# Adding the low word of a float64 weight to the bits of a float32 as an integer

## The chip, the cores and the metric

The kernel runs on one core of a Trainium2 chip. The metric is the device time of one execution in microseconds. The engines are named as in the profile: PE is TensorE, PEld its weight load, DVE is VectorE, ACT is ScalarE, POOL is GpSimd, SP is SyncE, which issues the DMAs.

## The reference

```python
X = np.fft.rfft(x, axis=1)                  # x: 2 x 3008 x 256, float32
Y = X * (filt_r + 1j * filt_i)[None]        # the filter: 1505 x 256
x = np.fft.irfft(Y, n=3008, axis=1).astype(np.float32).reshape(6016, 256)
h = x @ moe_w_in                            # 256 x 2048
x = ((np.maximum(h, 0) + alpha * np.minimum(h, 0)) @ moe_w_out).astype(np.float32)
h = np.maximum(x @ moe2_w_in, 0.0)
return (h * h @ moe2_w_out).astype(np.float32)
```

The four weight matrices (256 x 2048 and 2048 x 256) arrive as float64: a float32 array was divided by a float64 square root.

## The kernel before, in words

The convolution of each batch is an FFT of length 3008 = 64 x 47 as matmuls (units of 16 channels, lines 229 to 289, and a last stage, `stage4`, lines 297 to 314). Two networks follow, m = 0 and m = 1, on six tiles of 512 or 448 tokens per batch. The hidden dimension is cut into 16 blocks f of 128. Each operand of a network's matmul is split into a high part, rounded to the fp32r type, and a low part, the rest; a product is three matmuls (high x high, high x low, low x high).

One **step** of the main loop is one (network, batch, tile, f): six matmuls of line 423 for the hidden block (`h_mm`), the activation (`h_act`: line 436 on ACT and line 437 on DVE in the first network, lines 439 and 440 on ACT in the second), the split of the result (`g_split`: line 453 on ACT, line 454 on DVE), and two steps later six matmuls of lines 468 to 470 (`o_mm`). Tiles come in pairs: after the first few steps of the program, which take f = 0 and 1 for one tile and then for the other, each f is used for the pair's two tiles, so a new f is needed every second step. `split_x` (lines 401 and 403) makes the xs operand of a tile out of the convolution's X.

`weights(m, f)` turns 128 x 512 float64 weights into float32 and splits them. Line 320 loads a block into a staging tile stg (five of them); a view of it gives the low and the high words. Line 327 scales the low words by 2^-52 on ACT, writing floats over them. Line 329 takes the absolute value of the high words, read as floats, into c; line 331 clamps it, line 333 shifts the bits by three and masks, line 335 puts the sign and the top exponent bit of the high word back. c is then a float32 whose last three mantissa bits are zero. Line 337 masks c's exponent (and sign) into s, line 339 multiplies that by the scaled low words, line 342 adds the product to c. Line 346 rounds c to the high part (Wh for the first network) on ACT, line 348 subtracts it for the low part (Wl), and line 354 stores both to DRAM on SP's queue, from where `fetch` (line 364) loads them each time the network in the Wh and Wl tiles changes. c and s come from the nine tf tiles.

The order on every engine is written out at build time by a small planner, `Order`: each task is a generator that yields the cost of its next instruction on an engine, the events that it needs and the tiles that it takes; the planner issues, among the tasks that fit, the one that can start first. Engines run their instructions in the order so written. Before the main loop it runs until the first tile's xs and the weights f = 0 to 3 (`EARLY`) are there, and fills TensorE with `warm`, matmuls on zeros (line 505), meanwhile. In the main loop it fills each step with other tasks up to a few microseconds ahead of TensorE (lines 549 to 562): the rest of stage 4 of batch 0 at first, weights f = 4 to 15, then the second network's weights and the convolution of batch 1. Where a step needs weights that aren't planned yet, it plans their tasks first (`h_mm`).

Of the kernel before, what the change touches and what calls it, by code (L numbers as in the profile page):

```python
# [14 lines left out]
AF = mybir.ActivationFunctionType  # L15
ALU = mybir.AluOpType
# [43 lines left out]
def f32v(ap):  # L60
    return ap.bitcast(F32)
# [80 lines left out]
def conv_mlp_mlp(ctx, tc, x, fil, wts, alp, cst, out):  # L142
    nc = tc.nc
    V, A, G, T, SP = nc.vector, nc.scalar, nc.gpsimd, nc.tensor, nc.sync
# [172 lines left out]
    def weights(m, f, after=()):  # L317
        _, end = yield {"S": 0.6}, after, [(stg, 1)]
        t = stg.take()
        SP.dma_start(t.bitcast(U32), wts[m, :, f * 1024:(f + 1) * 1024])  # L320
        mark(("w", m, f), od.moved(end, 128 * 4096))
        w = t.bitcast(U32).rearrange("p (n w) -> p w n", w=2)
        low, high = w[:, 0, :], w[:, 1, :]
        yield {"A": 0.6}, [("w", m, f)], [(tf, 2)]
        c_, s_ = tf.take(), tf.take()
        c, s = c_.bitcast(U32), s_.bitcast(U32)
        A.activation(f32v(low), low, AF.Copy, scale=2.0 ** -52)
        yield {"A": 0.6}, [], []
        A.activation(c_, f32v(high), AF.Abs)
        yield {"V": 0.41}, [], []  # L330
        V.tensor_scalar(c_, c_, TINY, HUGE, op0=ALU.max, op1=ALU.min)
        yield {"V": 0.41}, [], []
        V.tensor_scalar(c, c, 3, 0x3FFFFFFF, op0=ALU.logical_shift_left, op1=ALU.bitwise_and)
        yield {"V": 0.67}, [], []
        V.scalar_tensor_tensor(c, high, 0xC0000000, c, op0=ALU.bitwise_and, op1=ALU.bitwise_or)  # L335
        yield {"V": 0.41}, [], []
        V.tensor_scalar(s, c, 0xFF800000, None, op0=ALU.bitwise_and)
        _, end = yield {"V": 0.68}, [], []
        V.tensor_mul(s_, s_, f32v(low))
        stg.give(end, t)  # L340
        _, end = yield {"V": 0.68}, [], []
        V.tensor_add(c_, c_, s_)  # L342
        tf.give(end, s_)
        _, end = yield {"A": 0.53}, [], [(tr, 2)] if m else []
        h, l = (tr.take(), tr.take()) if m else (WH[f], WL[f])
        A.copy(h, c_)  # L346
        _, end = yield {"V": 0.68}, [], []
        V.tensor_sub(l, c_, f32v(h))  # L348
        tf.give(end, c_)
        if not m:  # L350
            mark(("W", 0, 0, f), end)
        for k, p in enumerate((h, l)):
            _, end = yield {"S": 0.6}, [], []
            SP.dma_start(WD[m][f][k], f32v(p))
            end = od.moved(end, 128 * 2048)
            if m:
                tr.give(end, p)
        mark(("WD", m, f), end)
# [148 lines left out]
    with tc.manual_schedule():  # L507
# [12 lines left out]
        od.add(*(c0.stage4(h, g) for g in range(3) for h in range(2)))  # L520
        od.add(split_x(0, 0, 0), split_x(0, 0, 1))
        od.add(*(weights(0, f) for f in range(EARLY)))
        ahead, late = [], [("WD", 1, NF - 4)]
        for u in range(NU):
# [11 lines left out]
        c0.bank.give(0.0, banks[7])  # L536
        tf.keep, tr.keep = KEEP_F, KEEP_R
        od.add(*(weights(0, f) for f in range(EARLY, NF)))
        od.add(*(c0.stage4(h, g) for g in range(3, 8) for h in range(2)))
        od.add(*(split_x(*k) for k in units[2:]), lead=1.0)  # L540
        od.add(*(weights(1, f, [("W", 0, 0, NF - 1), ("xs", 0, 0, 3)]) for f in range(NF)))
        od.add(*ahead)
        t5 = len(TILES) - 1
# [99 lines left out]
```

## Time and profile before

| | |
|---|---|
| runs of the kernel | 1172.55, 1174.91, 1175.22 us (median 1174.91) |
| profiled execution | 1174.51 us, of which the span is 1172.7 us |
| mean granted TensorE clock | 0.996 |
| PE busy | 1153.8 us (98%) |
| DVE busy | 679.6 us (58%), 1067 instructions |
| ACT busy | 707.2 us (60%), 1258 instructions |
| POOL busy | 46.1 us (4%) |

The span goes from the first instruction to the last; the rest of the execution's time lies around it. Busy times count overlaps of an engine's own instructions once, so that a row's listed duration can be longer than the distance to the next instruction's start. Matmul ends are modelled. In a row of instructions the time in front is the start in microseconds from the span's start; an idle time in brackets stands with what ended it.

### The profile page before, as it was taken

The page shows a single profiled execution, that of the slowest core. Times are in us where ns is not written, and L with a number is a line of the kernel's source. Part 1 is how long each engine was busy: PE and PEld are TensorE (multiplying, and loading weights), DVE is VectorE, ACT ScalarE, POOL GpSimd, SP SyncE. Part 2 cuts the span into 40 slices and gives each one's busy share as a digit, 9 for nine tenths or more (in the row PEclk, how much of TensorE's full clock was granted, in tenths as well). Part 3 has the DMA queues.
Part 4 walks back from the last instruction along what each step waited for, and adds up shares of the span by engine and source line. Part 5 has one row for each costly group of instructions (what it writes and reads, how often), then busy time and mean ns, then how long its engine had stood idle before and what let it go on. Part 6 is the DMA issues. An engine that isn't in the chain of part 4 may idle for free.

```text
span 1172.7 us, 14233 instructions
## 1 busy us (share of the span) xinstructions
PE 1153.8 (98%) x5196; PEld 951.7 (81%) x5198; DVE 679.6 (58%) x1067; ACT 707.2 (60%) x1258; POOL 46.1 (4%) x52
## 2 busy tenths in 40 slices
PE   9999979999999999999999999999999999999998
PEld 4568658888888888888888888888888888888887
DVE  6788867888887776277622555655655322322322
ACT  1366636556667667666666644544544767767765
POOL 5400000000000110001000000000000000000000
PEclk9999989999999999999999999999999999999999
DMA  7653313323654122021223200000123100000000
GB/s 217 188 195 112 125 63 131 94 91 122 198 179 144 50 54 77 1 66 30 78 85 104 92 1 1 1 1 1 52 92 109 36 1 1 36 1 1 37 1 34
DMA packets 38007, 85.02 MB, mean 72 GB/s; under 512 B 4400, under 2 KB 5168, under 8 KB 37936
## 3 DMA queue, kind: packets, MB, share of 16 engines
q1 hardware_dynamic: 37936, 84.10, 22.3%
q8 instruction: 41, 0.67, 0.2%
q14 instruction: 30, 0.25, 0.1%
HBM read 61.15 MB, written 22.94 MB: 72 GB/s over the span
## 4 chain that ended last, share of the span: by engine, by line
PE 92%; DVE 3%; DMA 2%; ACT 1%; issue 1%; POOL 1%; POOLq 0%; ACTq 0%; SPq 0%
PE bank L423 43%; PE bank L468 14%; PE bank L470 14%; PE bank L469 14%; PE bank L308 2%; DMA stg<-in_fil 1%; PE bank L218 1%; PE bank L225 1%; PE bank L223 1%; PE bank L224 1%; DVE Wl L348 1%; DVE tf L437 1%; DVE tf L335 0%; DVE tf L342 0%; ACT tf L436 0%
## 5 line engine op out<-in xcount | busy, mean ns | idle before, releaser
L423 PE MATMUL bank<-xs,Wh 128*128 128x512 f32 (+1 forms) x1536 | 472.0, 388 | 4.1 <-ACT Wh L346 4.1
L454 DVE TENSOR_TENSOR tr<-tf,tr 128x512 fp32r<-128x512 f32 (+1 forms) x384 | 263.2, 685 | 352.9 <-ACT tr L453 348.7
L423 PEld LDWEIGHTS bank<-xs,Wh 128*128 128x128 f32 x1536 | 286.4, 188 | 58.4 <-ACT Wh L346 6.3
L453 ACT CAST tr<-tf 128x512 fp32r<-128x512 f32 (+1 forms) x384 | 234.9, 612 | 118.8 <-DVE tf L437 114.3
L423 PE MATMUL bank<-xs,Wl 128*128 128x512 f32 (+1 forms) x768 | 297.8, 388 | 5.7 <-DVE Wl L348 5.7
L468 PE MATMUL bank<-tr,Wh 128*128 128x512 f32 (+1 forms) x768 | 299.0, 389 | 0.0
L470 PE MATMUL bank<-tr,Wh 128*128 128x512 f32 (+1 forms) x768 | 297.3, 387 | 0.0
L469 PE MATMUL bank<-tr,Wl 128*128 128x512 f32 (+1 forms) x768 | 296.8, 386 | 0.0
L439 ACT ACTIVATE tf<-bank 128x512 f32<-128x512 f32 x192 | 113.2, 590 | 151.4 <-PE bank L423 151.2
L437 DVE SCALAR_TENSOR_TENSOR tf<-tf,one_minus_alpha,bank 128x512 f32<-128x512 f32 x192 | 141.3, 736 | 81.0 <-ACT tf L436 79.2
L436 ACT ACTIVATE tf<-bank 128x512 f32<-128x512 f32 x192 | 113.3, 590 | 120.3 <-PE bank L423 120.0
L423 PEld LDWEIGHTS bank<-xs,Wl 128*128 128x128 f32 x768 | 144.5, 188 | 36.1 <-DVE Wl L348 9.2
L470 PEld LDWEIGHTS bank<-tr,Wh 128*128 128x128 f32 x768 | 144.6, 188 | 27.8 <-DVE tr L454 0.3
L468 PEld LDWEIGHTS bank<-tr,Wh 128*128 128x128 f32 x768 | 144.7, 188 | 26.0
L469 PEld LDWEIGHTS bank<-tr,Wl 128*128 128x128 f32 x768 | 144.9, 189 | 25.7
L440 ACT ACTIVATE tf<-tf 128x512 f32<-128x512 f32 x192 | 119.7, 623 | 6.1
L200 POOL TENSOR_TENSOR stg<-stg,cst 128x384 f32<-128x384 f32 x32 | 30.5, 955 | 497.4 <-DMA Wl<-w 292.2
L308 PEld LDWEIGHTS bank<-cst,X 128*128 128x128 f32 x256 | 37.5, 190 | 8.3 <-ACT X L312 2.8
L287 DVE STREAM_TRANSPOSE X<-bank 128x512 f32<-128x512 f32 x32 | 34.7, 1089 | 11.1 <-PE bank L225 5.5
L403 DVE TENSOR_TENSOR xs<-X,xs 128x512 fp32r<-128x512 f32 (+1 forms) x48 | 32.5, 676 | 14.2 <-ACT xs L401 12.3
L308 PE MATMUL bank<-cst,X 128*128 128x94 f32 x256 | 36.8, 268 | 2.8 <-ACT X L312 2.2
L243 DVE STREAM_TRANSPOSE tf<-bank 128x512 f32<-128x512 f32 x32 | 22.8, 714 | 10.8 <-PE bank L218 6.9
(56 smaller groups left out, 573.6 us busy)
## 6 DMA issues: line engine op xcount, KB each, us to landing
stg<-in_wts SPq DMA_DIRECT2D x32, 512.0 KB, 4.0
stg<-in_fil SPq DMA_DIRECT2D x32, 384.0 KB, 3.5
Wh<-w SPq DMA_DIRECT2D x48, 256.0 KB, 2.6
Wl<-w SPq DMA_DIRECT2D x48, 256.0 KB, 2.9
w<-tr SPq DMA_DIRECT2D x32, 256.0 KB, 2.0
stg<-in_x SPq DMA_DIRECT2D x16, 384.0 KB, 4.2
out<-tf SPq DMA_DIRECT2D x20, 256.0 KB, 2.2
w<-Wh SPq DMA_DIRECT2D x16, 256.0 KB, 2.0
```

Source lines behind the costliest of these rows:

```text
L287: V.transpose(self.us[h].rearrange("p (i u d) -> p u d i", i=PR, u=8)[:, u % 8], pad(ps))
L308: T.matmul(ps[:, i * 94:i * 94 + 94], src[:, q], cs[:, O4:NCST], start=True, stop=True)
L423: T.matmul(ps[:, :n], w, r, start=(j == 0), stop=(j == 5))
L436: A.activation(q[:, :n], ps, AF.Relu, scale=-1.0)
L437: V.scalar_tensor_tensor(p[:, :n], q[:, :n], oma[:, f:f + 1], ps, op0=ALU.mult, op1=ALU.add)
L439: A.activation(q[:, :n], ps, AF.Relu)
L440: A.activation(p[:, :n], q[:, :n], AF.Square)
L453: A.copy(gh[:, :n], p[:, :n])
L454: V.tensor_sub(gl[:, :n], p[:, :n], f32v(gh[:, :n]))
L468: T.matmul(ps[:, :n], WH[f][:, w], gh[:, :n], start=(f == 0), stop=False)
L469: T.matmul(ps[:, :n], WL[f][:, w], gh[:, :n], start=False, stop=False)
L470: T.matmul(ps[:, :n], WH[f][:, w], gl[:, :n], start=False, stop=(f == NF - 1))
```

## The change

The low word, scaled by 2^-29, is an integer of 0 to 8 once it is rounded: what the three empty mantissa bits of c lack, with a carry. Line 327 now writes it as an integer into s, and one addition on the 32-bit patterns of c and s stands in place of mask, product and float sum. The staging tile is given back after line 335 instead of after line 339, and the planner's costs follow the new instructions.

```diff
-        A.activation(f32v(low), low, AF.Copy, scale=2.0 ** -52)
+
+        A.activation(s, low, AF.Copy, scale=2.0 ** -29)
         yield {"A": 0.6}, [], []
         A.activation(c_, f32v(high), AF.Abs)
...
-        yield {"V": 0.67}, [], []
+        _, end = yield {"V": 0.67}, [], []
         V.scalar_tensor_tensor(c, high, 0xC0000000, c, op0=ALU.bitwise_and, op1=ALU.bitwise_or)
-        yield {"V": 0.41}, [], []
-        V.tensor_scalar(s, c, 0xFF800000, None, op0=ALU.bitwise_and)
-        _, end = yield {"V": 0.68}, [], []
-        V.tensor_mul(s_, s_, f32v(low))
         stg.give(end, t)
-        _, end = yield {"V": 0.68}, [], []
-        V.tensor_add(c_, c_, s_)
+        _, end = yield {"V": 0.69}, [], []
+
+        V.tensor_add(c, c, s)
         tf.give(end, s_)
```

## Rows read from the trace of the kernel before

**Rows 1.** The page, busy us, share of the span and instructions of each engine

```profile
PE 1153.8 (98%) x5196; PEld 951.7 (81%) x5198; DVE 679.6 (58%) x1067; ACT 707.2 (60%) x1258; POOL 46.1 (4%) x52
```

**Rows 2.** Stretches of 20 us: length, busy by engine, PEclk, DMA share, GB/s

```profile
140.00:160.00 20.00, 14.56 (x53) 10.32 (x51) 15.91 (x30) 9.41 (x16) 0.00 (x0) 0.91 0.15 54
160.00:180.00 20.00, 17.32 (x66) 13.09 (x65) 12.24 (x21) 7.97 (x14) 0.00 (x0) 0.91 0.32 109
180.00:200.00 20.00, 20.00 (x90) 16.57 (x89) 16.00 (x27) 13.34 (x24) 0.00 (x0) 1.00 0.29 105
```

**Rows 3.** Waits of PE from 66 to 178 us: total us, times, longest

```profile
PE bank L423 <- DVE Wl L348: 5.7, 8, 1.5
PE bank L423 <- ACT Wh L346: 4.1, 3, 3.1
PE bank L308 <- ACT X L312: 2.2, 2, 1.5
```

**Rows 4.** PE's timeline: first matmuls of steps (start us, us)

```profile
93.29 0.71 PE L423 MATMUL bank<-xs,Wh 128*128 128x512 f32 x2
...
96.93 0.71 PE L423 MATMUL bank<-xs,Wh 128*128 128x512 f32 x2
...
110.21 0.62 PE L423 MATMUL bank<-xs,Wh 128*128 128x512 f32 x2
...
112.93 0.62 PE L423 MATMUL bank<-xs,Wh 128*128 128x512 f32 x2
...
121.09 0.61 PE L423 MATMUL bank<-xs,Wh 128*128 128x512 f32 x2
...
178.65 0.62 PE L423 MATMUL bank<-xs,Wh 128*128 128x512 f32 x2
```

**Rows 5.** Groups by line: count, busy us, mean ns, idle before

```profile
L337 DVE TENSOR_SCALAR tf<-tf 128x512 uint32<-128x512 uint32 x32 | 13.4, 421 | 0.0
L339 DVE TENSOR_TENSOR tf<-tf,stg 128x512 f32<-128x512 f32 x32 | 21.9, 685 | 0.0
L342 DVE TENSOR_TENSOR tf<-tf,tf 128x512 f32<-128x512 f32 x32 | 21.9, 685 | 0.0
L209 DVE TENSOR_TENSOR tr<-tf,tr 128x384 fp32r<-128x384 f32 x32 | 18.1, 567 | 2.1 <-ACT tr L207 1.6
L327 ACT ACTIVATE stg<-stg 128x512 f32<-128x512 uint32 x32 | 21.5, 673 | 1.5 <-DMA stg<-in_wts 1.5
```

**Rows 6.** DVE's timeline from 144.7 us (start us, us)

```profile
144.74 0.42 DVE L331 TENSOR_SCALAR tf<-tf 128x512 f32<-128x512 f32 x1
145.08 0.69 DVE L339 TENSOR_TENSOR tf<-tf,stg 128x512 f32<-128x512 f32 x1
145.68 0.69 DVE L454 TENSOR_TENSOR tr<-tf,tr 128x512 fp32r<-128x512 f32 x1
146.28 0.68 DVE L342 TENSOR_TENSOR tf<-tf,tf 128x512 f32<-128x512 f32 x1
146.89 0.74 DVE L437 SCALAR_TENSOR_TENSOR tf<-tf,one_minus_alpha,bank 128x512 f32<-128x512 f32 x1
147.54 0.42 DVE L333 TENSOR_SCALAR tf<-tf 128x512 uint32<-128x512 uint32 x1
```

**Rows 7.** DVE's and PE's timeline ahead of the main loop

```profile
56.54 0.41 DVE L337 TENSOR_SCALAR tf<-tf 128x512 uint32<-128x512 uint32 x1
...
63.33 0.70 DVE L403 TENSOR_TENSOR xs<-X,xs 128x512 fp32r<-128x512 f32 x1
...
71.84 0.69 DVE L348 TENSOR_TENSOR Wl<-tf,Wh 128x512 fp32r<-128x512 f32 x1 [0.68 <-ACT Wh L346]
...
61.44 6.85 PE L505 MATMUL bank<-zeros 128*128 128x512 bf16 x31
...
68.50 0.70 PE L423 MATMUL bank<-xs,Wh 128*128 128x512 f32 x2
```

**Rows 8.** Waits of ACT from 68 to 178 us: total us, times, longest

```profile
ACT tf L436 <- PE bank L423: 26.0, 22, 3.4
```

## The prediction

> **What bounds the kernel now.** I read the page's busy shares first: TensorE is busy 1153.8 of 1172.7 us, VectorE only 58% of it [rows 1]. So a change on VectorE and ScalarE can only be worth what TensorE loses by waiting or by filler work. The table of 20 us stretches finds the first part of that: all loss lies before 180 us, and from 140 to 180 us TensorE is busy 14.56 and 17.32 of 20 us at a granted clock of 0.91 [rows 2]; from 180 us on every stretch is full, as the third row. The waits of TensorE in 66 to 178 us then name what is late: the matmuls of line 423 wait 5.7 us in 8 waits for Wl (line 348) and 4.1 us for Wh (line 346), and the stage-4 matmuls of line 308 wait 2.2 us for a copy on ScalarE [rows 3]. Wl and Wh of the first network are what weights() delivers, so the disputed work is on the path that sets the end.
>
> What these waits cost I take from the step starts, since a wait also leaves an empty pipeline and a low clock behind. An undisturbed step is 112.93 - 110.21 = 2.72 us. From 121.09 to 178.65 us there are 15 steps (16 to 30, counted on the timeline), 57.56 us where 15 x 2.72 = 40.80 would do: **16.8 us lost** [rows 4]. One f has two steps, and eight f (8 to 15) wait, as the 8 waits say.
>
> Why is Wl late? VectorE's timeline shows when each instruction gives way to the next, which is shorter than its listed duration: a tensor_scalar 0.34 us, a two-tensor instruction 0.60, line 437 0.65 [rows 6]. One f takes two steps of lines 437 and 454 (2 x 1.25 = 2.50 us) and one block of weights: three tensor_scalar (1.02) and four two-tensor instructions (2.40), together 5.92 us. TensorE needs 2 x 2.72 = 5.44 for the same f. **In the short steps VectorE is the slower of the two by 0.48 us per f**; in the earlier long steps, with stage 4 between them (96.93 - 93.29 = 3.64 us, 7.28 per f), it gains 1.36 per f, and that lead is used up at f = 8.
>
> The second part is the start. The main loop can't be earlier than 31 warm-up matmuls allow, 6.85 us from 61.44 us (0.221 each) [rows 7]. Their number is not a wait: the planner writes as many as fit until, in its own costs, blocks 0 to 3 are done. The last xs part of the first tile starts at 63.33 us on VectorE and takes 0.70, so the data are there some 4 us before the warm-up ends [rows 7].
>
> **The change part by part.** *Removed:* line 337 (421 ns, 32 of them) and line 339 (685 ns, 32) [rows 5], in giving-way time 0.34 + 0.60 = 0.94 us per block [rows 6].
>
> *Replaced:* the float sum of line 342 becomes a sum of two uint32 tiles. No row shows that instruction. Low end: like a single-source one, 421 ns. High end within one instruction: each word taken as two 16-bit halves, 1024 elements instead of 512. From 128x384 at 567 ns and 128x512 at 685 ns an element costs 118/128 = 0.92 ns, so 685 + 512 x 0.92 = 1157 ns [rows 5]. I take 685 ns, because the instruction has the same two sources, destination and words as line 342 now. Toward the low end nothing more is won, since TensorE is the slower one by then; the high end is a rival.
>
> The Trainium skill, VectorE: DVE Perf Modes, section Specifications, says that the engine computes in float32, that integer operands are converted and that results are exact only below 2^24. By that an exact sum of 32-bit patterns can't be one plain pass; no row here shows either. One pass that rounds would give the time of the sum below; several passes give the slower rival.
>
> *Kept but redirected:* the ScalarE copy of line 327 writes s, as an integer, and no longer overwrites the low words. Nearest row: 673 ns for the same 512 columns out of uint32 [rows 5]. I cost it at nothing, and what covers it is ScalarE's idle time, 26.0 us of waiting for TensorE at line 436 alone in 68 to 178 us [rows 8]. Its ends are 0 and, at twice the duration and without that cover, 0.67 us once, in the start's last block.
>
> *Moved:* stg is given back after line 335, two or more instructions earlier, so the weight loads of line 320 on SyncE's queue can go earlier, ahead of the line 354 stores they stand between. ScalarE waits for such a load once at line 327, 1.5 us [rows 5]. I take nothing for it, with 0 and -1.5 as ends. No wait is added.
>
> *The written order:* the planner's VectorE cost of a block falls from 3.94 (0.41 + 0.41 + 0.67 + 0.41 + 3 x 0.68) to 2.86 (0.41 + 0.41 + 0.67 + 0.69 + 0.68), by 1.08. With 2 x (0.75 + 0.62) = 2.74 for two steps, a plan for one f was 6.68 against a planned 5.2 of TensorE, and is now 5.60.
>
> **Term 1, the start.** From 56.54 to 71.84 us VectorE runs practically without a gap and holds lines 337 and 339 of all four early blocks [rows 7]. Planned, that is 4 x 1.08 = 4.3 us, 19 or 20 warm-ups; really 4 x 0.94 = 3.7 us. As the first data already lie some 4 us ahead of the end of the warm-up and come earlier too, the plan's number decides. I take 4.0, with 3.5 to 4.3 as ends; what could eat into it is the tail of block 3, cast on ScalarE and then line 348, with less other work around it.
>
> **Term 2, the stalls.** VectorE's need per f falls to 5.92 - 0.94 = 4.98 us, below TensorE's 5.44. In the long steps the lead grows by 2.3 us instead of 1.4 per f, in the short ones it should no longer shrink. In the plan it still shrinks by 0.4 per f, some 3 us over eight f, which the larger lead of the long steps covers. I leave 2 us for waits at the last f's, since the instructions stand in a fixed order and a block's tail can stand behind a line 437 that waits for TensorE: 16.8 - 2 = 14.8 us back.
>
> **Term 3,** the 2.2 us at line 308 during steps 0 to 2: the copy there stands behind block 3's cast and a weight load; both come earlier by about as much as the steps do. Nothing, with 0 to -2.2 as ends.
>
> What is late next: nothing after 180 us waits now, so the time saved stays saved; work of the second convolution and the second network's weights moves with the steps.
>
> **The sum,** against the profiled execution, 1174.5 us (span 1172.7 plus 1.8 around it, 0.4 below the median of 1174.9): 1174.5 - 4.0 - 14.8 = **1155.7 us**. All ends favourable: 1174.5 - 4.3 - 16.8 - 2.2 = 1151.2.
>
> **The rivals.**
> *Half the stalls stay.* The order is written out, so an instruction free to run stands behind one that waits. For it: VectorE is busy only 12.24 of 20 us from 160 to 180 us, where Wl is latest [rows 2], so not raw capacity alone makes it late. Against it: that idleness comes after TensorE stopped, a consequence. 1174.5 - 4.0 - 8.4 = 1162.1.
> *The sum takes two half-words per word.* Giving way after about 1.07 us (1157 less the 0.085 us by which 685 exceeds 0.60), VectorE's f is 4.98 - 0.60 + 1.07 = 5.45, level with TensorE's 5.44. A third of the stalls, 5.6 us, would stay: 1174.5 - 4.0 - 11.2 = 1159.3.
> *Slower: the exact sum is several passes.* Place: between line 335 and the cast of line 346, on VectorE. What it replaces gave way after 0.34 + 0.60 + 0.60 = 1.54 us, so above that each block is slower than before. With four two-tensor passes, 2.40 us, it is 0.86 more per block, 12 x 0.86 = 10.3 us over blocks 4 to 15, while some 2 us of the start would still be won: 1183 us. The page named above speaks for it; the planner's cost of 0.69 in the diff, that of one pass, speaks against it.
> *It does nothing to the end:* Wl is late for another reason, such as its loads. The one 1.5 us wait for a load says no. 1174.5.
>
> **How the numbers follow.** Forecast 0.65, half the stalls 0.20, two half-words 0.07, nothing 0.03, several passes 0.05. A measurement can tell 0.3% here, 3.5 us; the first three cases all lie beyond it. So faster 0.92, same 0.03, slower 0.05. The range goes from 1151 (all ends favourable) to 1163 (half the stalls with the start's low end, 1162.6); the predicted time is the forecast's, rounded to 1156.
>
> **What would show it.** VectorE has 64 instructions fewer, 1003, and some 35 us less busy time (13.4 + 21.9 [rows 5]); the new sum stands at about 685 ns. The warm-up row falls from 31 to 11 to 15 matmuls, and the first matmul of line 423 moves from 68.50 [rows 7] to about 64.5 us. The waits of line 423 for lines 346 and 348 fall from 9.8 us to 2 or less, the step starts of f = 8 to 15 lie 2.72 us apart, and the clock stays at 1.00 in every stretch. I am wrong if the sum takes over 1.07 us, if line 423 still waits at most f's, or if a wait as long appears after 180 us.

## The result, and the profile after

The changed kernel takes **1156.26 us** (median of 4 runs, 1155.40 to 1157.32) against 1174.74 us: a ratio of 0.9847, 95% interval 0.983 to 0.9864, 18.5 us less. The forecast was 1156 us, faster. The profiled execution took 1157.10 us, its span 1155.2. The changed kernel's lines 328 to 336 are 327 to 335 of before, its line 340 is the sum, and what follows is two lower: 346 is 344, 348 is 346, 423 is 421, 437 is 435, 454 is 452, 505 is 503.

The page, busy time of each engine, answers to [rows 1]; VectorE has the 64 instructions less and 29.5 us less busy time (I had expected some 35 from the listed durations; the giving-way times, 32 x 0.94 = 30.1 us, come nearer, as busy time counts overlaps once):

```profile
PE 1146.1 (99%) x5182; PEld 949.4 (82%) x5184; DVE 650.1 (56%) x1003; ACT 707.3 (61%) x1258; POOL 45.3 (4%) x52
```

The 20 us stretches (busy by engine, clock, DMA share) answer to [rows 2]. TensorE is full where it had lost most, at full clock:

```profile
140.00:160.00 20.00, 20.00 (x90) 16.57 (x89) 15.23 (x24) 10.85 (x19) 0.00 (x0) 1.00 0.47 167
160.00:180.00 20.00, 20.00 (x90) 16.57 (x89) 15.95 (x26) 14.45 (x27) 0.00 (x0) 1.00 0.16 57
```

The waits of TensorE from 60 to 178 us answer to [rows 3]. Both kinds of wait for weights are gone, and what is left is the one of stage 4 for a copy, 2.1 us against 2.2 before:

```profile
PE bank L308 <- ACT X L312: 2.1, 1, 2.1
```

The groups of the two redirected instructions answer to [rows 5]. The sum is one instruction on 16-bit halves, and hardly slower than the float sum (703 against 685 ns); line 328 costs what line 327 did:

```profile
L340 DVE CUSTOM_DVE_ANT_0 tf<-tf,tf 128x1024 uint16<-128x1024 uint16 x32 | 22.4, 703 | 0.0
L328 ACT ACTIVATE tf<-stg 128x512 uint32<-128x512 uint32 x32 | 21.3, 667 | 1.9 <-DMA stg<-in_wts 1.9
```

VectorE's timeline has two of these sums in a row, then another instruction 1.20 us after the first: 0.60 us each until the next may start, as the float sum in [rows 6].

```profile
62.22 1.28 DVE L340 CUSTOM_DVE_ANT_0 tf<-tf,tf 128x1024 uint16<-128x1024 uint16 x2
63.42 0.68 DVE L401 TENSOR_TENSOR xs<-X,xs 128x512 fp32r<-128x512 f32 x1
```

PE's timeline (last warm-ups, then first matmuls of steps 0, 1, 2, 16 and 31) answers to [rows 4, 7]:

```profile
63.40 3.83 PE L503 MATMUL bank<-zeros 128*128 128x512 bf16 x17
...
67.43 0.71 PE L421 MATMUL bank<-xs,Wh 128*128 128x512 f32 x2
...
70.02 0.71 PE L421 MATMUL bank<-xs,Wh 128*128 128x512 f32 x2
...
74.23 0.70 PE L421 MATMUL bank<-xs,Wh 128*128 128x512 f32 x2
...
119.80 0.62 PE L421 MATMUL bank<-xs,Wh 128*128 128x512 f32 x2
...
160.60 0.62 PE L421 MATMUL bank<-xs,Wh 128*128 128x512 f32 x2
```

From step 16 to step 31 it takes 40.80 us, 15 x 2.72, where it took 57.56. But the main loop begins only 1.07 us earlier, with 14 warm-ups less in the written order (40 instead of 54). Something ahead of it came later. VectorE's first transpose, which waits for the convolution's first matmuls (line 218), shows it; the row of before is the first, of after the second:

```profile
7.44 3.29 DVE L243 STREAM_TRANSPOSE tf<-bank 128x512 f32<-128x512 f32 x4 [6.31 <-PE bank L218]
```

```profile
9.10 3.29 DVE L243 STREAM_TRANSPOSE tf<-bank 128x512 f32<-128x512 f32 x4 [7.97 <-PE bank L218]
```

Two theories were to be told apart. The prediction's, **engine time**: the weights came late because VectorE needed 5.92 us per f against TensorE's 5.44, and they come in time because it needs 4.98 now. The rival, **written order**: what counts is where a block's instructions stand among the steps, and that is set by the planner's costs, which the diff lowers together with the work.

### The profile page after: what moved, and what is told of

Read it like the earlier page. It is cut to its first block, busy times and chain, and to the rows that moved or that the text cites. A ratio compares the mean times of both kernels' runs of the same rounds, so it can differ in the third digit from the quotient of the medians.

```text
span 1155.2 us, 14144 instructions
## 1 busy us (share of the span) xinstructions
PE 1146.1 (99%) x5182; PEld 949.4 (82%) x5184; DVE 650.1 (56%) x1003; ACT 707.3 (61%) x1258; POOL 45.3 (4%) x52
## 4 chain that ended last, share of the span: by engine, by line
PE 95%; DMA 2%; DVE 1%; POOL 1%; ACT 0%; issue 0%; SPq 0%; POOLq 0%; ACTq 0%
PE bank L421 44%; PE bank L466 15%; PE bank L468 15%; PE bank L467 15%; PE bank L308 2%; DMA stg<-in_fil 1%; PE bank L218 1%; DMA stg<-in_wts 1%; PE bank L225 1%; PE bank L223 1%; PE bank L224 1%; PE bank L503 0%; POOL tf L261 0%; PE bank L510 0%; POOL stg L200 0%
## 5 line engine op out<-in xcount | busy, mean ns | idle before, releaser
L401 DVE TENSOR_TENSOR xs<-X,xs 128x512 fp32r<-128x512 f32 (+1 forms) x48 | 32.4, 674 | 17.5 <-ACT xs L399 15.6
```

## The experiments

The table cuts every profiled span at three points of PE's and VectorE's timelines: first transpose, step 0, step 31, end (us). Times are medians with the ratio to runs of the kernel before on the same chip. Run 10, whose early steps differ, is told in the text.

| | time, ratio (95%) | first transpose | to step 0 | step 0 to 31 | to the end |
|---|---|---|---|---|---|
| before | 1174.74 | 7.44 | 61.06 | 110.15 | 994.05 |
| after | 1156.26, 0.9847 (0.983 to 0.9864) | 9.10 | 58.33 | 93.17 | 994.60 |
| 1 after again | 1155.40, 0.9841 (0.9827 to 0.9856) | 8.85 | 57.37 | 92.95 | 994.53 |
| 2 order only | 1165.07, 0.9925 (0.991 to 0.994) | 8.38 | 58.10 | 100.55 | 997.17 |
| 3 work only | 1171.57, 0.9978 (0.9969 to 0.9988) | 8.75 | 60.80 | 105.54 | 994.51 |
| 4 early blocks only | 1172.63, 0.9991 (0.9982 to 1.0001) | 8.11 | 57.34 | 110.36 | 994.09 |
| 5 late blocks only | 1157.96, 0.9868 (0.9852 to 0.9884) | 7.65 | 60.38 | 93.20 | 994.07 |
| 6 second network only | 1174.74, 1.0004 (0.9995 to 1.0014) | 9.03 | 60.37 | 109.08 | 994.82 |
| 7 before, lower costs | 1167.01, 0.9949 (0.9933 to 0.9965) | 7.54 | 60.09 | 102.83 | 994.84 |
| 8 after, lower costs | 1157.78, 0.9867 (0.9852 to 0.9881) | 8.46 | 57.12 | 93.63 | 996.69 |
| 9 EARLY = 3 | 1152.89, 0.9818 (0.9804 to 0.9833) | 9.04 | 55.92 | 92.61 | 994.93 |
| 11 fewer warm-ups | 1155.85, 0.9847 (0.9831 to 0.9864) | 7.84 | 55.50 | 92.65 | 995.01 |
| 12 sum twice | 1156.93, 0.9851 (0.9836 to 0.9866) | 8.18 | 57.13 | 94.80 | 994.99 |

**1. The same kernel again.** No edit.

> The changed kernel once more, for a second profile. In the first one the main loop began only 1.07 us earlier (67.43 instead of 68.50 us) with 14 warm-up matmuls less (14 x 0.221 = 3.1 us), while VectorE's first transpose came 1.66 us later (9.10 instead of 7.44 us). Theory 'load': the first load's landing varies from execution to execution; then the time is 1155 to 1157.5 us, and start of the main loop minus start of the first transpose stays at about 58.3 us whatever the landing. Rival 'order': the changed order costs the convolution time; then the first transpose comes at 9.1 us again and the main loop begins at 67.4 us again.

The loop began at 66.22 us with the first transpose at 8.85. Over all fourteen profiles the first transpose lies anywhere from 7.44 to 9.10 us, also in kernels whose order up to there is that of before (run 3: 8.75, run 6: 9.03). So this moment varies from execution to execution, and 1.66 of the 1.07 + 1.66 = 2.73 us by which the start had moved were hidden by it.

It is not the load that varies, though. The first load is issued at 0.7 us and lands 4.2 us later in the kernel before and 3.8 us later in the changed one, so it is the earlier one where the transpose is the later; over all profiles it takes 3.7 to 4.3 us. What the transpose waits for is line 218 on TensorE, and that stands, without idle time, behind ten matmuls on zeros that take 2.32 us in the kernel before (first two rows) and 3.63 us in the changed one (last two):

```profile
4.22 2.32 PE L505 MATMUL bank<-zeros 128*128 128x512 bf16 x10
6.38 3.60 PE L218 MATMUL bank<-stg,cst 96*128 96x512 f32 x8
```

```profile
4.58 3.63 PE L503 MATMUL bank<-zeros 128*128 128x512 bf16 x10
8.04 3.60 PE L218 MATMUL bank<-stg,cst 96*128 96x512 f32 x8
```

The traces' first record of a granted clock of 1.00 stands at 3.85 us in the kernel before and at 7.21 us in the changed one; these matmuls start 0.43 us apart ahead of it and 0.22 behind it. In all fourteen profiles the transpose comes the later, the later this record does. TensorE's work up to there starts at 1.19 us in each and is the same, but for one matmul less in run 11; why the clock rises earlier in one execution than in another, no run shows. The distance from transpose to step 0 is not as fixed as I expected either (57.37 against 58.33 us); I did not follow where that difference arises.

**2. Only the order.** The three old instructions stand where the integer sum stood, at its planned cost; the staging tile is given back behind them.

```diff
-        yield {"V": 0.41}, [], []
+        _, end = yield {"V": 0.69}, [], []
         V.tensor_scalar(s, c, 0xFF800000, None, op0=ALU.bitwise_and)
-        _, end = yield {"V": 0.68}, [], []
         V.tensor_mul(s_, s_, f32v(low))
-        stg.give(end, t)
-        _, end = yield {"V": 0.68}, [], []
         V.tensor_add(c_, c_, s_)
+        stg.give(end, t)
```

> All eight instructions of before, written in the order that the planner's cheaper costs give (mask, product and float sum stand together where the integer sum stood, at 0.69 us of plan). Theory 'engine time': VectorE still needs 5.92 us per f, so the stalls at f = 8 to 15 stay at 15 to 20 us; 14 warm-ups fewer start the loop up to 3 us earlier, which the stalls give back in part: 1170 to 1175 us. Rival 'written order': the order alone takes the stalls away: 1156 to 1161 us.

It gains half of the change, outside both ranges. VectorE's and ScalarE's instructions stand in exactly the order of the changed kernel, with three in place of the one sum. Of TensorE's waits from 60 to 182 us none is for Wh or Wl any more, and steps 16 to 31 take 40.8 us as in the changed kernel, although VectorE still has 5.92 us of work per f:

```profile
PE bank L308 <- ACT X L312: 3.6, 1, 3.6
PE bank L421 <- DVE tf L435: 1.2, 2, 0.8
PE bank L421 <- DVE xs L401: 0.5, 1, 0.5
PE bank L468 <- DVE tr L452: 0.5, 1, 0.5
```

It is in fact somewhat more than 5.92. Mask, product and sum now stand one behind the other, and each reads what the one ahead of it wrote. They start 0.45 and 0.73 us apart, where [rows 6], with other instructions between them, show 0.34 and 0.60; that is 0.24 us more per block:

```profile
112.35 0.42 DVE L337 TENSOR_SCALAR tf<-tf 128x512 uint32<-128x512 uint32 x1
112.80 0.69 DVE L338 TENSOR_TENSOR tf<-tf,stg 128x512 f32<-128x512 f32 x1
113.53 0.69 DVE L339 TENSOR_TENSOR tf<-tf,tf 128x512 f32<-128x512 f32 x1
```

What it doesn't gain goes another way: the blocks now crowd VectorE, and TensorE waits for activations (lines 435 and 452) and for a copy behind block 3's cast. Up to step 31 that costs 100.55 - 93.17 = 7.4 us. Of these, 4.3 are lost before step 2: TensorE waits 3.6 us for that copy, the granted clock falls to 0.50 meanwhile and stays there until 77.4 us:

```profile
73.00:75.00 2.00, 1.63 (x6) 1.53 (x7) 1.34 (x3) 2.00 (x6) 0.00 (x0) 0.50 1.01 373
```

The other 3.1 are lost in steps 9 to 14, around the waits for activations. Another 2.6 us are lost after step 31, where the second network's blocks do the same: from 180 to 340 us VectorE is 92% busy and TensorE 158.84 us of 160, where in the changed kernel (second row) VectorE is 85% busy and TensorE all the time:

```profile
180.00:340.00 160.00, 158.84 (x716) 133.58 (x715) 146.89 (x249) 96.08 (x174) 3.69 (x4) 1.00 0.47 149
180.00:340.00 160.00, 160.00 (x729) 136.28 (x728) 135.50 (x221) 99.96 (x179) 3.58 (x4) 1.00 0.48 153
```

**3. Only the work.** The changed instructions in the order of before: two planned costs stay, with nothing issued.

```diff
-        _, end = yield {"V": 0.67}, [], []
+        yield {"V": 0.67}, [], []
         V.scalar_tensor_tensor(c, high, 0xC0000000, c, op0=ALU.bitwise_and, op1=ALU.bitwise_or)
+        yield {"V": 0.41}, [], []
+        _, end = yield {"V": 0.68}, [], []
         stg.give(end, t)
-        _, end = yield {"V": 0.69}, [], []
+        _, end = yield {"V": 0.68}, [], []
```

> The changed instructions in the order and with the planner's costs of before (the two removed instructions are planned and not issued). Theory 'engine time': the start stays (54 warm-ups), the stalls fall from 16.8 us to between 0 and 5 us: 1158 to 1163 us. Rival 'written order': the blocks' ends stand behind the same lines 437 as before, the stalls stay over 12 us: 1169 to 1175 us.

Inside the rival's range: 2.3 us, an eighth of the change. VectorE's and ScalarE's order is exactly that of before, without the two instructions. Steps 16 to 31 take 54.13 us, so 13.3 of the 16.8 us stay lost. TensorE's waits for weights from 60 to 182 us are 7.7 us, against 9.8 in [rows 3]:

```profile
PE bank L423 <- DVE Wl L348: 4.2, 5, 1.5
PE bank L423 <- ACT Wh L346: 3.5, 3, 3.1
```

VectorE's timeline says why a faster block is not an earlier one. These are its instructions from 112.33 us to the end of block 8 (an idle time and its cause in brackets):

```profile
112.33 0.75 DVE L437 SCALAR_TENSOR_TENSOR tf<-tf,one_minus_alpha,bank 128x512 f32<-128x512 f32 x1 [0.31 <-ACT tf L436]
113.76 0.69 DVE L454 TENSOR_TENSOR tr<-tf,tr 128x512 fp32r<-128x512 f32 x1 [0.69 <-ACT tr L453]
115.05 0.75 DVE L437 SCALAR_TENSOR_TENSOR tf<-tf,one_minus_alpha,bank 128x512 f32<-128x512 f32 x1 [0.59 <-ACT tf L436]
116.48 0.69 DVE L454 TENSOR_TENSOR tr<-tf,tr 128x512 fp32r<-128x512 f32 x1 [0.69 <-ACT tr L453]
117.09 0.69 DVE L342 CUSTOM_DVE_ANT_0 tf<-tf,tf 128x1024 uint16<-128x1024 uint16 x1
117.77 0.75 DVE L437 SCALAR_TENSOR_TENSOR tf<-tf,one_minus_alpha,bank 128x512 f32<-128x512 f32 x1
118.43 0.68 DVE L336 SCALAR_TENSOR_TENSOR tf<-stg,tf 128x512 uint32<-128x512 uint32 x1
119.20 0.69 DVE L454 TENSOR_TENSOR tr<-tf,tr 128x512 fp32r<-128x512 f32 x1
120.43 0.75 DVE L437 SCALAR_TENSOR_TENSOR tf<-tf,one_minus_alpha,bank 128x512 f32<-128x512 f32 x1 [0.53 <-ACT tf L436]
121.09 0.68 DVE L348 TENSOR_TENSOR Wl<-tf,Wh 128x512 fp32r<-128x512 f32 x1
```

Lines 336 and 342 are 335 and the sum here. From 112.33 to 117.09 us, almost two steps, no instruction of a block is there at all, and VectorE idles (0.69, 0.59, 0.69 us); then line 348 of block 8, which step 16 needs, stands behind the line 437 of a step before, which waits for ScalarE, which waits for TensorE. In the planner's costs VectorE presumably had no room earlier; run 7 bears that out: with lower costs and the work of before, line 348 of block 8 starts at 109.59 us. In the changed kernel the instructions stand closer, with two or three of a block in each step:

```profile
104.04 0.69 DVE L346 TENSOR_TENSOR Wl<-tf,Wh 128x512 fp32r<-128x512 f32 x1 [0.19 <-ACT Wh L344]
104.65 0.69 DVE L336 SCALAR_TENSOR_TENSOR tf<-stg,tf 128x512 uint32<-128x512 uint32 x1
105.25 0.74 DVE L435 SCALAR_TENSOR_TENSOR tf<-tf,one_minus_alpha,bank 128x512 f32<-128x512 f32 x1
105.91 0.69 DVE L340 CUSTOM_DVE_ANT_0 tf<-tf,tf 128x1024 uint16<-128x1024 uint16 x1
106.51 0.42 DVE L332 TENSOR_SCALAR tf<-tf 128x512 f32<-128x512 f32 x1
106.85 0.69 DVE L452 TENSOR_TENSOR tr<-tf,tr 128x512 fp32r<-128x512 f32 x1
107.45 0.69 DVE L346 TENSOR_TENSOR Wl<-tf,Wh 128x512 fp32r<-128x512 f32 x1
```

The two line 346 here are the ends of blocks 8 and 9 (the ninth and tenth of them on the timeline): block 8 is done at 104.7 us, 17 us before run 3's.

The earlier give-back of the staging tile has no run to itself. Run 2 gives it back later in the plan than the changed kernel and has no wait for weights either.

**4, 5 and 6. Parts of the blocks.** Both variants of weights() in one kernel, each block by a condition.

```diff
+        if m == 0 and f < EARLY:
...
+        else:
```

with `m == 0 and f >= EARLY` in run 5 and `m == 1` in run 6.

> Only blocks f = 0 to 3 of the first network are changed, the other 28 are as before. Theory 'two separate terms': the start comes 3 us earlier (40 warm-ups instead of 54), the stalls at f = 8 to 15 stay at 16 to 20 us: 1170 to 1173 us. Rival 'one shared lead': what the early blocks save is only a lead that the later blocks use up, so an earlier start is given back in full at f = 8: 1174 to 1176 us.

> Only blocks f = 4 to 15 of the first network are changed; the four early ones and the second network's are as before. 54 warm-ups, so the start stays. Theory 'order and work of these twelve blocks': the stalls at f = 8 to 15 go altogether, 14 to 17 us: 1157 to 1160 us. Rival 'the lead comes from the early blocks': half of the stalls stay, 1164 to 1168 us.

> Only the sixteen blocks of the second network are changed. No wait of TensorE stood after 180 us before, so nothing is to be had: 1172.5 to 1175.5 us, the stalls at f = 8 to 15 as before. Rival: the second network's blocks cost steps of TensorE without a visible wait (the order-only run lost 5 us after step 31): 1168 to 1171 us.

The early blocks alone start the loop 61.06 - 57.34 = 3.7 us sooner after the first transpose, yet only 1.2 us of that reach the measured time, with an interval that touches no change. The time is in the first theory's range, near its end, and so is the profile, whose stretch to step 31 is as long as before (110.36 us); but the timed runs show less than the 3 us expected, so this run alone settles little. The late blocks alone bring 16.5 us: 1157.96 is in the range, no wait for weights is left, and the stretch is 93.20 us. The second network's blocks bring nothing, as expected: after step 31 nothing waited. (The order-only run lost 2.6 us after step 31, not the 5 named in the rival.)

**7 and 8. Only the planner's costs.** No instruction is changed. Run 7 is the kernel before with the distances that [rows 6] show as its block's planned costs, 3.42 in place of 3.94 us; run 8 the same for the changed kernel, 2.48 in place of 2.86.

```diff
-        yield {"V": 0.41}, [], []
+        yield {"V": 0.34}, [], []
...
-        yield {"V": 0.67}, [], []
+        yield {"V": 0.6}, [], []
...
-        _, end = yield {"V": 0.68}, [], []
+        _, end = yield {"V": 0.6}, [], []
```

> The instructions of before; only the planner's costs of the seven VectorE instructions of a block are set to what the trace shows as giving-way time (0.34 and 0.60 instead of 0.41, 0.67 and 0.68; a block 3.42 instead of 3.94). 49 warm-ups instead of 54. Theory 'written order' (a block's planned cost decides where it stands among the steps): about half of the plan's change, so the start 1 us earlier and 5 to 12 us of the stalls gone: 1161 to 1168 us. Rival 'engine time': 1171 to 1174 us.

> The changed kernel with a block's planned cost set to giving-way times (0.34, 0.34, 0.60, 0.60, 0.60: 2.48 instead of 2.86). 36 warm-ups instead of 40, so the start 0.9 us earlier; there are no stalls to win. Theory 'the start is what is left': 1153.5 to 1155.5 us. Rival 'a plan too tight' (as in the order-only run, TensorE then waits for lines 435 and 452 behind the blocks): 1157 to 1161 us.

Run 7 wins 7.4 us without any change of the work, in the range of the written order. TensorE's waits for weights fall to 4.0 us:

```profile
PE bank L423 <- ACT Wh L346: 2.4, 1, 2.4
...
PE bank L423 <- DVE Wl L348: 1.6, 3, 0.8
```

Run 8 goes too far and lands in the rival's range: the loop starts sooner, and step 2 then waits 2.3 us for an activation. That costs little, as it takes the place of the changed kernel's 2.1 us wait for a copy. But waits for xs from 240 to 280 us follow, and 2.1 us are lost after step 31.

```profile
PE bank L421 <- DVE tf L435: 2.3, 1, 2.3
...
PE bank L421 <- DVE xs L401: 0.8, 2, 0.5
```

**9, 10 and 11. The start.** Runs 9 and 10 are the changed kernel with fewer blocks planned ahead of the loop, run 11 with warm-ups planned longer than they are.

```diff
-EARLY = 4
+EARLY = 3
```

(2 in run 10), and in run 11

```diff
-            _, end = yield {"T": 0.22}, [], []
+            _, end = yield {"T": 0.3}, [], []
```

> The changed kernel with EARLY = 3: the main loop is planned to begin when blocks 0 to 2 are there, 28 warm-ups instead of 40. Block 3 is needed only at step 6. Theory 'the plan's warm-ups set the start': up to 12 x 0.221 = 2.7 us earlier, limited by the first tile's xs, which ends 1.5 us ahead of the loop in the changed kernel: 1153 to 1155.5 us. Rival 'the data set the start': 1155.5 to 1157 us, the gain waited out in steps 0 to 2.

> The same with EARLY = 2, 25 warm-ups. Theory 'the plan's warm-ups set the start': 1152.5 to 1155 us. Rival: the early steps wait for blocks 2 and 3 on VectorE, 1156 to 1160 us.

> The changed kernel with a warm-up planned at 0.30 us instead of 0.22, and nothing else: 31 warm-ups instead of 40. They really take 0.221, so TensorE is free 2.0 us sooner. Theory 'the warm-ups set the start': 1.0 to 1.6 us faster than the changed kernel (as far as the first xs and Wl allow), 1153.5 to 1155 us. Rival 'the data set it': the same time as the changed kernel, 1155 to 1156.5 us.

Run 9 is the fastest of all, 1152.89 us, just under the range: its loop starts 55.92 us after the first transpose, 2.4 and 1.5 us less than in the changed kernel's two profiles, and two waits of 1.0 us in all for Wl come back late in the stretch. Its ratio, 0.9818, lies 0.0029 under the changed kernel's, with intervals that just overlap. Run 10 is slower than the changed kernel, 1166.25 us (ratio 0.9932, 0.9918 to 0.9947): steps 3 to 4 are 8.64 us apart instead of 3.64, and the waits for Wl are back:

```profile
PE bank L421 <- DVE Wl L346: 8.5, 5, 2.5
```

Run 11 is inconclusive: its profiled execution, 1152.73 us, began the loop 55.50 us after the first transpose, but the other runs spread from 1155.67 to 1157.99 us, and its ratio is that of the changed kernel.

**12. The sum twice.** A second integer sum behind the first, into a tile that nothing reads, at no planned cost.

```diff
         V.tensor_add(c, c, s)
+        V.tensor_add(s, s, s)
```

> The changed kernel with a second integer sum behind each one (s + s into s, which nothing reads), not known to the planner: what the change would be if the exact sum took two instructions. VectorE then needs 5.58 us per f against TensorE's 5.44. Theory 'the order carries it, VectorE only has to keep up': no wait for Wl at f = 8 to 15, but 1 to 6 us of waits for activations: 1156.5 to 1162 us. Rival 'engine time' (what the prediction argued with): above 5.44 the waits for Wl come back, a third of the 16.8 us or more: 1161 to 1168 us.

VectorE's 5.58 us per f (5.7 by this trace, where the second sum starts 0.72 us after the first) exceed TensorE's 5.44, and yet there is no wait for Wh or Wl. The time is at the favourable end of the order's range; the stretch to step 31 is 1.6 us longer, 1.3 of them before step 2.

```profile
L341 DVE CUSTOM_DVE_ANT_0 tf<-tf 128x1024 uint16<-128x1024 uint16 x32 | 22.7, 710 | 1.1
L340 DVE CUSTOM_DVE_ANT_0 tf<-tf,tf 128x1024 uint16<-128x1024 uint16 x32 | 21.9, 683 | 0.0
```

## Why the prediction was right, and where it wasn't

**What bounds the kernel: right.** All that was won lies before step 31; the rest of the span differs by 0.6 us. The lost time of steps 16 to 31, 16.8 us, came back whole.

**Term 1, the start: too large.** I took 4.0 us, because "the plan's number decides" and the plan saves 4 x 1.08 = 4.3. That the plan decides is right: with the old work and 40 warm-ups the loop begins 58.10 us after the transpose (run 2), with the new work and 54 warm-ups 60.80 (run 3). But the plan saved only 14 warm-ups, 14 x 0.221 = 3.1 us; on average, the five profiles with 40 warm-ups (after, runs 1, 2, 4 and 12) lie 3.0 us below the four with 54 (before, runs 3, 5 and 6). Runs 7 and 8 show the same: 2.1 us of planned cost saved there are 5 warm-ups, 1.5 us are 4, where 9 and 7 would do. A part of a planned saving seems to become idle time in the plan; which instruction it waits for there, I did not look into.

**Term 2, the stalls: too small by 2 us, and for a reason that doesn't hold.** I left 2 us of 16.8 and none stayed. The step that failed is the cause: "In the short steps VectorE is the slower of the two by 0.48 us per f". As a balance of work it is right, but it does not make the weights late. By its own numbers it wouldn't do so at f = 8: the long steps 4 to 9 (f = 2 to 4) gain 3 x 1.36 = 4.1 us, and f = 6 and 7 use up 2 x 0.48 = 1.0 of them before f = 8, where I let the lead end. In the trace of before VectorE idles for 4.1 of the 38.72 us of steps 4 to 15, while TensorE is busy throughout, and the lead is not worn down but lost within one block. The last instruction of block 7 ends 7.7 us before step 14, which begins at 115.65 us and needs it; that of block 8 starts only after step 16 has begun, at 121.09:

```profile
107.28 0.69 DVE L348 TENSOR_TENSOR Wl<-tf,Wh 128x512 fp32r<-128x512 f32 x1
...
121.22 0.68 DVE L348 TENSOR_TENSOR Wl<-tf,Wh 128x512 fp32r<-128x512 f32 x1
```

The runs agree. With 5.92 us per f in the new order no weight is waited for (run 2), with 5.58 neither (run 12), and with 4.98 in the old order 7.7 us of waits and 13.3 us of the lost time stay (run 3). What the runs show in its place is the written order, which I had only as a supporting sentence ("a plan for one f was 6.68 against a planned 5.2 of TensorE, and is now 5.60"): lower planned costs put a block's last instruction steps earlier in VectorE's queue. The work matters as the other half: in the new order the old instructions cost 1165.07 - 1155.40 = 9.7 us (run 2), by crowding out activations and, before step 2, a stage-4 copy. So the two halves of the diff need each other: 2.3 us by the work alone, 8.8 by the order alone, 18.5 together.

**Term 3: right,** 2.2 us at line 308 before and 2.1 after. **The sum,** 1155.7 us, came within 0.6 us of the median, and partly by luck. Terms 1 and 2 missed in opposite directions, by 0.9 and 2.0 us. In the profiled execution 2.73 us are saved up to step 0 and 16.98 up to step 31; the clock's late rise at the start takes 1.66 back and the rest of the span 0.55, which leaves the 17.5 us by which the spans differ.

**The cost of the integer sum: right by the float sum's row, wrong in its high end.** I priced halves at 0.92 ns each, 1157 ns in all. They took 703: 1024 halves in the time of 512 words. The Trainium skill, VectorE: DVE Perf Modes, section The perf-mode tier table, lists `tensor_tensor` on bf16 in SBUF at 2x and on float32 at 1x. This row, a custom instruction on uint16, agrees with that ratio, and I had not carried it over to the halves. Of the page's sentence on exactness below 2^24 the trace shows only that no plain 32-bit pass stands there; no run looks at the sum's bits. In any case one instruction did it, so the slower rival, several passes, fell. My limit of 1.07 us for the sum is not borne out by run 12 either, where two sums take 1.33 us of VectorE (0.72 until the second starts, 0.61 until the next instruction).

**Half the stalls stay** named the right mechanism, a free instruction behind one that waits; it is run 3's, and the changed order removed it here.

## What to carry to other kernels

Where an order is written by a planner, an instruction that is removed has two effects, and the planned one can be the larger: test them apart, by keeping the cost without the instruction and the instruction without the cost. Costs that are a little above what the engine needs can make it wait in its own queue, and costs below it crowd out what other engines wait for; the distance between starts, not the listed duration, is the time to compare with. A balance of work per step says whether an engine can keep up, not whether a given result is early enough: for that, follow the result's last instruction and what it stands behind.

## What was unexpected

A sum of uint32 words costs VectorE hardly more than a float sum: 703 ns for 128x512 words, as 128x1024 halves, and 0.60 us until the next instruction. The moment at which TensorE's granted clock first rises (3.85 to 7.21 us) alone moves an execution by up to 1.7 us (first transpose at 7.44 to 9.10 us), which is more than run 11 was to show in one profile. And the weights' planned start has a sharp limit: three early blocks instead of four gain some 3 us, with intervals that just overlap, and two lose 10.
